# A decode kernel with 80 transfers in place of 88: two head records laid down keys first and loaded together

## The chip, the core and the metric

The kernel runs on one core of one Trainium2 chip. The metric is device time in microseconds (us), the median of the runs. A core has engines that work side by side, each through its own instructions in program order: PE (matrix products), DVE (vector work), ACT (exponentials and copies), POOL, and SP, which here only issues transfers from the chip's memory (HBM) into the core's memory (SBUF). A transfer that SP issues is carried out by 16 DMA engines, each with a part of the 128 partitions, and transfers of one queue are served in the order of their issue. Engines wait for each other, and for transfers, through semaphores; a reader waits for the whole transfer that brings its data.

## The reference, cut to what matters

Two rounds of the same two layers, with the same weights: attention of one new token over the last 1024 positions of a cache with 32 heads, and an MLP with relu. Batch 4, width 640, head size 128, hidden width 1728, all float32.

```python
x = x + _A_ref(_layernorm(x), A_k_cache, A_v_cache, A_wq, A_wo)
x = x + _B_ref(_layernorm(x), B_w1, B_w2)
x = x + _A_ref(_layernorm(x), A_k_cache, A_v_cache, A_wq, A_wo)
x = x + _B_ref(_layernorm(x), B_w1, B_w2)

# _A_ref, W = 1024
q = (x @ wq).reshape(B, Sq, Hq, Dh).transpose(0, 2, 1, 3)
k, v = k_cache[:, :, Sk - W:, :], v_cache[:, :, Sk - W:, :]
p = softmax(einsum("bhqd,bhkd->bhqk", q, k) * Dh ** -0.5)
o = einsum("bhqk,bhkd->bhqd", p, v)
return o.transpose(0, 2, 1, 3).reshape(B, Sq, Hq * Dh) @ wo

# _B_ref
return maximum(x @ w1, 0) @ w2
```

## The kernel before, in words

**Records.** The host lays down all that one head needs as a record of 9472 columns on 128 partitions: its part of `wq` (640 columns, from `WQ`), its keys (4096, from `K` = 640), its values (4096, from `V` = 4736) and its part of `wo` (640, from `WO` = 8832). A record is 4736 KB; "keys of a head" below means columns 0 to `V`, query weights among them, 2368 KB, and "rest" the other half. `wm` holds the MLP's weights in the order of their use.

**Rounds.** The first round (`r` = 0) goes through heads 0 to 31. The last five, 27 to 31, stay in SBUF, and the second round (`r` = 1) begins with them and then takes 0 to 26, so its last three heads are 24, 25 and 26. Five records fit into the tile `store`; a small tile `kept` holds a part of record 26 over the rounds, from column `KEPT` = 6784, and `ring` and a part of record 31's place serve the MLP's weights of the first round.

**Transfers.** A list `items` holds all loads in order, built ahead of the computation (`load`, `run`, `piece`, `group`, `weight`, `ending`). `pump` emits the next loads on SP as soon as the program has released the columns that they overwrite (`done` and `free` release them, at the point of the program where their last reader stands). SP takes them strictly in this order. Most records come five at a time in three transfers (`FIVE`). Towards the end of a round they come in smaller pieces (`ending`), keys ahead of the rest. In the first round's MLP (`MLP_RING`) each load waits for the computation to free its place, and at the start of the second round (`places`) the loads fill the gaps that single released pieces leave. In between, `park` copies four pieces of record 31 into PSUM to make room, and `unpark` copies them back into the freed places of record 27's keys.

**One step of the head loop** (lines 513 to 538). For head `n` PE runs, in this order: the scores of head `n + 1`, the values of head `n`, the query of head `n + 2`, the transposed output of head `n` (`output_T`, into `t_ps`), and head `n`'s projection into `acc` (at once in the second round, except for its last two heads, and held back for the last six of the first). DVE and ACT run the softmax of head `n + 1` beside it. At the last step (`end`) four fills, matrix products whose result nobody reads (`busy`), stand between the values and the last query, and the last head's scores follow that query at once. After the loop come the last two heads' values and projections, layer norm (`center`, `deviation`) and the MLP (`mlp`): the first product over `w1` into `sc_ps`, relu on DVE into `scratch`, the second product over `w2` into `acc`. The final copy and the store end the program.

All operations go through one helper, so the profile puts nearly all of them on its line 102 and tells them apart by their tiles: `misc` is a query, `sc_ps<-store,qT` are scores, `o_ps<-store,scratch` values, `t_ps` the transposed output, `acc<-store,oTs` a projection, `acc<-kept,small` a fill, `acc<-store,scratch` the second product of the second round's MLP.

Of the kernel before, what the change touches and what calls it, by code (L numbers as in the profile page):

```python
# [38 lines left out]
P = 128  # L39
B, D, H, DH, W, FF = 4, 640, 32, 128, 1024, 1728  # L40
# [6 lines left out]
WQ, K, V, WO = 0, D, D + 4 * W, D + 8 * W  # L47
REC = 2 * D + 8 * W
HALF = REC // 2
VH = 2 * W  # L50
# [9 lines left out]
KEPT = WO - 4 * 512  # L60
# [12 lines left out]

IN_RING = [(2176, 4736, "spare", 0), (4736, 6272, "ring", 0), (6272, 8832, "ring", 1536)]

CUTS = [*range(0, K, DH), *range(K, WO, 512), *range(WO, REC + 1, FD)]
W1_SLOT = [[0, 1], [2, 3], [4]]
W2_SLOT = [22, 20, 8, 4]
LATE = 6


FIVE = [REC + 6272, 2 * REC - 3072, 2 * REC - 3200]
LAST_FIVE = [REC + 4736, 2 * REC - 4736, REC, REC]
THREE = [REC + HALF, REC + HALF]
GROUPS = [{h: FIVE for h in range(0, 25, 5)}, {6: THREE, 9: FIVE, 14: FIVE, 19: LAST_FIVE}]


class InOrder:
# [21 lines left out]
def decode_kernel(ctx: ExitStack, tc: tile.TileContext, xf, rec, wm, out):  # L110
# [25 lines left out]
    store = sb.tile([P, FIRST + NS * REC], F32, name="store")  # L136
    kept = sb.tile([P, REC - KEPT], F32, name="kept")
# [39 lines left out]
    LAST = H - NS  # L177


    def home(h, r):  # L180

        if r:
            return FIRST + (h if h >= LAST else h - 6 + LAST) % NS * REC
        return (0 if h < NS else FIRST) + h % NS * REC
# [8 lines left out]
    def load(src, lo, hi, buf, col, parts):  # L193
        items.append((src[:, lo:hi], buf, col, hi - lo, parts))
# [4 lines left out]
    def weight(r, lo, hi, buf, col):  # L199
        buf, col = place(buf, col)  # L200
        load(wm, lo, hi, buf, col, [(("w", r), lo, hi, col)])


    def run(r, lo, hi, buf, col):
        parts = [(("rec", r, h), max(lo - h * REC, 0), min(hi - h * REC, REC), col + max(h * REC - lo, 0))
                 for h in range(lo // REC, (hi - 1) // REC + 1)]
        load(rec, lo, hi, buf, col, parts)

    def piece(r, h, lo, hi, buf="store", col=None):
        run(r, h * REC + lo, h * REC + hi, buf, home(h, r) + lo if col is None else col)  # L210


    def group(r, h, sizes):
        lo = 0
        for size in sizes:
            run(r, h * REC + lo, h * REC + lo + size, "store", home(h, r) + lo)
            lo += size

    def ending(r, hs, late):
        a, b, c = hs[-3:]  # L220
        end = WO if late else REC
        for h, lo, hi in ((a, 0, V), (b, 0, V), (a, V, end), (c, 0, V), (b, V, end), (c, V, WO if late else KEPT)):
            piece(r, h, lo, hi)
        if late:
            for h in hs[-1:] + hs[-LATE:-1]:
                if h == LAST - 1:
                    piece(r, h, WO, REC, "kept", WO - KEPT)
                else:
                    piece(r, h, WO, REC)
# [3 lines left out]
    for h in hs[:-3]:  # L233
        if h in GROUPS[0]:
            group(0, h, GROUPS[0][h])
        if h >= 25:
            piece(0, h, 0, KEPT if h == LAST - 1 else WO if h >= H - LATE else REC)
        if h == LAST - 1:
            piece(0, h, KEPT, WO, "kept", 0)
    ending(0, hs, True)  # L240
    for lo, hi, buf, col in MLP_RING:
        weight(0, lo, hi, buf, col)
# [7 lines left out]
    for lo, hi, buf, col in IN_RING:  # L250
        piece(1, new[0], lo, hi, *place(buf, col))
    places = [("store", old[i] + lo, old[j] + hi) for i, lo, j, hi in (
        (0, 0, 0, K), (0, K + 1024, 0, K + VH), (0, K + VH + 1536, 0, V), (1, 0, 1, K), (1, K, 1, K + VH), (1, K + VH, 1, V),
        (0, V, 0, WO), (2, 0, 2, V), (1, V, 1, REC), (3, 0, 3, V), (2, V, 2, REC), (3, V, 4, FROM))]
    places += [("store", 0, FIRST), ("store", old[4] + FROM, old[4] + REC), ("ring", 0, RING)]
    cuts = [h * REC + x for h in new[1:6] for x in CUTS]
    c, end = new[1] * REC, new[6] * REC
    for buf, lo, hi in places:
        if lo == old[1]:
            piece(1, new[0], WO, REC, buf, lo)  # L260
        elif c < end:
            cut = max(x for x in cuts if x <= min(end, c + hi - lo))
            run(1, c, cut, buf, lo)
            c = cut
    assert c == end
    for h in new[6:-3]:
        if h in GROUPS[1]:
            group(1, h, GROUPS[1][h])
        if not any(g <= h < g + sum(z) // REC for g, z in GROUPS[1].items()):
            piece(1, h, 0, REC)  # L270
    ending(1, hs, False)
    for ks in W1_SLOT:
        weight(1, ks[0] * FF, (ks[-1] + 1) * FF, "store", home(LAST + 1, 0) + ks[0] * FF)
# [54 lines left out]

    def unpark(i):
        b = home(LAST, 0)  # L330
        a = b + (K, K + 512, K + VH, K + VH + 512, K + VH + 1024)[i]
        copy = dve.tensor_copy if i in (0, 2) else act.copy
        copy(store[:, a:a + 512], (sc_ps[1][:, :512], sc_ps[1][:, 512:], o_ps, misc, t_ps)[i])
        live.append(("store", a, a + 512))
        if i == 2:
            dve.memset(o_ps, 0.0)
        if i == 4:
            c = spare
            at["rec", 1, H - 1] = [(0, FROM, "store", c), (FROM, V, "store", a - 512), (V, V + 1024, "store", b + K),
                                   (V + 1024, V + 1536, "store", b + K + VH), (V + 1536, REC, "store", c + V + 1536)]  # L340


    h_ps, warm = sc_ps[0][:, :512], sc_ps[0][:, 512:]
# [55 lines left out]
    def scores(r, h, s, first=False):  # L399
        key = ("rec", r, h)  # L400
        for i in range(2):
            for b in range(B):
                pe.matmul(sc_ps[s][32 * b:32 * b + 32, 512 * i:512 * i + 512], qT[:, b:b + 1].to_broadcast([P, 32]),
                          cols(key, K + 512 * (B * i + b), 512), start=True, stop=True)
            done(key, K + VH * i, K + VH * i + VH)
            if first and i == 0:
                if r:
                    unpark(0)
                deviation(eps_dh, float(DH), True)
                act.activation(unused, eps, AF.Exp)  # L410
                if r:
                    unpark(1)
# [87 lines left out]
    for r in range(2):  # L500
        hs = order[r]
        late = LATE if r == 0 else 2
# [6 lines left out]
        if r:  # L509
            unpark(2)  # L510
            unpark(3)
        weights(0, ((0, 1), (1, 2)))
        for n, h in enumerate(hs[:-2]):
            i = n - (H - late)
# [5 lines left out]
            end = n == H - 3  # L520
# [82 lines left out]
```

## Time and profile before

| | |
|---|---|
| median of 3 runs | 711.71 us (711.58 to 711.9) |
| the profiled execution | 712.25 us |
| its span, first to last instruction | 710.5 us |
| share of the span in which PE, DVE, ACT are busy | 72%, 41%, 14% |
| share of the DMA engines' time that the queue of loads takes | 98.9% |
| read from HBM | 301.34 MB, 424 GB/s over the span |
| mean granted clock of PE | 0.803 of full speed |

The profile is of one execution. Busy shares are means over the whole span and say little where the limit changes from stage to stage: the attention of the first round reaches to about 365 us, its MLP to about 393, the second round's attention to about 693, its MLP to the end. The granted clock is the share of full speed that PE had; here it is 1.00 or 0.50 at any one time. In a timeline row the first number is the start in us from the span's start, the second the length; `x16` joins 16 instructions, and the brackets give the engine's idle time just before and what ended it.

### The profile page before, as it was taken

To read this page: it belongs to the slowest core of one execution; us is meant where nothing else is said; L and a number is where in the kernel's file an instruction comes from. 1 tells how busy PE (TensorE), PEld (TensorE's weight loads), DVE (VectorE), ACT (ScalarE), POOL (GpSimd) and SP (SyncE) were. 2 spreads that over 40 slices of the span, in tenths; PEclk is the share of its full clock that TensorE was granted. 3 is DMA by queue.
4 is the path that set the end of the run, shared out by engine and by line. 5 is a ranking of instruction groups with operands and counts; after the bars stand their busy time and mean duration, and the time that the engine had idled before them with its cause. 6 is when DMAs were issued, how large, how long until landed. Compare 5 with 4: busy or idle time off the path is not lost.

```text
span 710.5 us, 8480 instructions
## 1 busy us (share of the span) xinstructions
PE 513.0 (72%) x3722; PEld 214.0 (30%) x3722; DVE 293.3 (41%) x518; ACT 99.7 (14%) x210; POOL 1.1 (0%) x9
## 2 busy tenths in 40 slices
PE   0777586677584578869888999656584678686986
PEld 0332232232331223333323443222241232332322
DVE  3242353243342343435531775525162243453651
ACT  0110110011010110111120422101010011011110
POOL 0000000000000000000000000000000000000000
PEclk9977787677778776877999999968597677777989
DMA  9999999999999999999999999999999999999996
GB/s 398 439 416 447 425 435 443 414 439 450 418 435 441 424 437 421 423 439 423 430 398 403 412 426 433 445 435 437 431 435 426 438 436 430 432 432 416 433 425 281
DMA packets 12596, 301.96 MB, mean 425 GB/s; under 512 B 1408, under 2 KB 1552, under 8 KB 4624
## 3 DMA queue, kind: packets, MB, share of 16 engines
q1 hardware_dynamic: 12528, 301.42, 98.9%
q8 instruction: 29, 0.48, 0.2%
q14 instruction: 7, 0.06, 0.0%
q10 hardware_dynamic: 32, 0.01, 0.0%
HBM read 301.34 MB, written 0.08 MB: 424 GB/s over the span
## 4 chain that ended last, share of the span: by engine, by line
DMA 72%; PE 23%; DVE 4%; issue 1%; ACT 1%; ACTq 0%; SPq 0%; DVEq 0%
DMA store<-rec 65%; PE sc_ps L102 9%; PE o_ps L102 6%; DMA store<-wm 4%; PE acc L102 3%; PE misc L102 3%; DMA ring<-wm 2%; DVE scratch L102 2%; PE t_ps L102 1%; DVE o_ps L102 1%; ACT oTs L102 1%; DVE small L102 0%; DVE sc_ps L102 0%; ACT sc_ps L102 0%; ACTq L102 0%
## 5 line engine op out<-in xcount | busy, mean ns | idle before, releaser
L102 PE MATMUL sc_ps<-store,qT 128*32 128x512 f32 x1024 | 194.5, 849 | 35.7 <-DMA store<-rec 34.3
L102 PE MATMUL misc<-xT,store 128*128 128x4 f32 x620 | 95.6, 281 | 109.8 <-DMA store<-rec 109.8
L102 DVE TENSOR_REDUCE small<-sc_ps 128x1 f32<-128x1024 f32 x64 | 78.4, 1224 | 181.3 <-PE sc_ps L102 181.2
L102 PE MATMUL o_ps<-store,scratch 128*16 128x512 f32 x960 | 149.5, 701 | 1.7 <-DMA store<-rec 1.4
L102 PEld LDWEIGHTS misc<-xT,store 128*128 128x128 f32 x620 | 90.2, 227 | 166.6 <-DMA store<-rec 119.4
L102 ACT ACTIVATE sc_ps<-sc_ps,small 128x1024 f32<-128x1024 f32 x64 | 69.8, 1091 | 322.6 <-DVE small L102 322.6
L102 DVE STREAM_TRANSPOSE sc_ps<-sc_ps 128x1024 f32<-128x1024 f32 (+1 forms) x70 | 80.8, 1155 | 0.1
L102 PEld LDWEIGHTS sc_ps<-store,qT 128*32 128x32 f32 x1024 | 41.5, 139 | 112.4 <-issue 60.7
L102 PEld LDWEIGHTS o_ps<-store,scratch 128*16 128x16 f32 x960 | 33.8, 117 | 117.4 <-issue 107.8
L102 DVE TENSOR_TENSOR o_ps<-o_ps,of_block 128x512 f32<-128x512 f32 x62 | 43.3, 699 | 50.6 <-PE o_ps L102 50.6
L102 DVE TENSOR_TENSOR qT<-misc,rows 128x4 f32<-128x4 f32 x61 | 9.5, 155 | 112.9 <-PE misc L102 112.9
L102 PE MATMUL acc<-store,oTs 128*4 128x160 f32 x488 | 34.1, 363 | 17.0 <-ACT oTs L102 17.0
L102 DVE TENSOR_REDUCE scratch<-o_ps 128x128 f32<-128x512 f32 x62 | 42.9, 691 | 2.1
L102 ACT COPY oTs<-t_ps 128x4 f32<-128x4 f32 x59 | 9.6, 163 | 207.4 <-PE t_ps L102 207.4
L102 PE MATMUL t_ps<-rows,scratch 128*128 128x4 f32 x118 | 25.8, 289 | 11.3 <-DVE scratch L102 10.3
L102 PEld LDWEIGHTS t_ps<-rows,scratch 128*128 128x128 f32 x118 | 21.9, 231 | 17.4 <-DVE scratch L102 13.1
L102 DVE SCALAR_TENSOR_TENSOR scratch<-sc_ps,small,of_batch 128x128 f32<-128x128 f32 (+1 forms) x70 | 23.7, 339 | 3.5 <-PE o_ps L102 0.9
L102 PE MATMUL acc<-kept,small 128*1 128x328 f32 (+2 forms) x54 | 17.7, 433 | 0.0
L102 PEld LDWEIGHTS acc<-store,oTs 128*4 128x4 f32 x488 | 7.1, 84 | 22.5 <-ACT oTs L102 22.1
L102 ACT ACTIVATION_READ_ACCUMULATOR sc_ps<-sc_ps,small 128x1 f32 x64 | 12.3, 193 | 0.0
L102 DVE RECIPROCAL small<-small 128x1 f32<-128x1 f32 x64 | 9.8, 153 | 2.3 <-ACT sc_ps L102 2.3
L102 PE MATMUL acc<-store,scratch 128*4 128x160 f32 x146 | 6.1, 299 | 3.3 <-DMA store<-wm 3.2
(83 smaller groups left out, 99.8 us busy)
## 6 DMA issues: line engine op xcount, KB each, us to landing
store<-rec SPq DMA_DIRECT2D x14, 7872.0 KB, 27.3
store<-rec SPq DMA_DIRECT2D x7, 7936.0 KB, 29.9
store<-rec SPq DMA_DIRECT2D x4, 7104.0 KB, 30.8
store<-rec SPq DMA_DIRECT2D x11, 2368.0 KB, 36.5
store<-rec SPq DMA_DIRECT2D x3, 4736.0 KB, 25.7
store<-rec SPq DMA_DIRECT2D x2, 4416.0 KB, 29.1
store<-rec SPq DMA_DIRECT2D x3, 2048.0 KB, 40.7
store<-rec SPq DMA_DIRECT2D x1, 4160.0 KB, 21.6
```

The lines of the kernel that those rows point to most:

```text
L102: r = build(*args, **kwargs)
```

## The change

The program's computation is the same; what changes is how the data lies in HBM and in which pieces it is loaded.

- Records 25 and 26 (`PAIR` and `PAIR + 1`) are laid down as one double record: keys of 25, keys of 26, rest of 25, rest of 26. In the first round all of it up to column `KEPT` of record 26 comes in one transfer of 65,024 bytes a partition. In the second round it comes in three: both heads' keys, the rest of 25, and the part of 26's values that `kept` doesn't hold.
- The third last head of a round (29 in the first, 24 in the second) comes in one transfer, up to `WO` in the first round. Before, its keys came first, the next head's keys second and its rest third.
- The last five records that the second round takes in groups (19 to 23) are cut like the others (`FIVE` in place of `LAST_FIVE`): three transfers in place of four.
- In the second round the MLP's `w1` comes in two transfers in place of three.
- At the start of the second round two pairs of places become one place each. `unpark` puts the parked pieces into the first 2560 columns of record 27's keys, behind the query weights, so that the 1536 columns up to `V` are free in one piece; the other pair is record 28's keys.

The longest row of a transfer was 63,488 bytes and is 65,024 bytes; the bytes loaded are the same.

```diff
@@ -73,16 +73,19 @@
 
 IN_RING = [(2176, 4736, "spare", 0), (4736, 6272, "ring", 0), (6272, 8832, "ring", 1536)]
 
+
+PAIR = H - 7
+PAIRED = [(PAIR, 0, V, 0), (PAIR + 1, 0, V, V), (PAIR, V, REC, 2 * V), (PAIR + 1, V, REC, V + REC)]
+
 CUTS = [*range(0, K, DH), *range(K, WO, 512), *range(WO, REC + 1, FD)]
-W1_SLOT = [[0, 1], [2, 3], [4]]
+W1_SLOT = [[0, 1, 2], [3, 4]]
 W2_SLOT = [22, 20, 8, 4]
 LATE = 6
 
 
 FIVE = [REC + 6272, 2 * REC - 3072, 2 * REC - 3200]
-LAST_FIVE = [REC + 4736, 2 * REC - 4736, REC, REC]
 THREE = [REC + HALF, REC + HALF]
-GROUPS = [{h: FIVE for h in range(0, 25, 5)}, {6: THREE, 9: FIVE, 14: FIVE, 19: LAST_FIVE}]
+GROUPS = [{h: FIVE for h in range(0, 25, 5)}, {6: THREE, 9: FIVE, 14: FIVE, 19: FIVE}]
 
 
 class InOrder:
@@ -210,6 +213,11 @@
         run(r, h * REC + lo, h * REC + hi, buf, home(h, r) + lo if col is None else col)
 
 
+    def pair(r, lo, hi):
+        parts = [(("rec", r, h), x + max(lo - a, 0), min(y, x + hi - a), home(PAIR, r) + max(lo, a))
+                 for h, x, y, a in PAIRED if lo < a + y - x and a < hi]
+        load(rec, PAIR * REC + lo, PAIR * REC + hi, "store", home(PAIR, r) + lo, parts)
+
     def group(r, h, sizes):
         lo = 0
         for size in sizes:
@@ -218,10 +226,13 @@
 
     def ending(r, hs, late):
         a, b, c = hs[-3:]
-        end = WO if late else REC
-        for h, lo, hi in ((a, 0, V), (b, 0, V), (a, V, end), (c, 0, V), (b, V, end), (c, V, WO if late else KEPT)):
-            piece(r, h, lo, hi)
-        if late:
+        if not late:
+            piece(r, a, 0, REC)
+            for lo, hi in ((0, 2 * V), (2 * V, V + REC), (V + REC, REC + KEPT)):
+                pair(r, lo, hi)
+        else:
+            for h, lo, hi in ((a, 0, WO), (b, 0, V), (c, 0, V), (b, V, WO), (c, V, WO)):
+                piece(r, h, lo, hi)
             for h in hs[-1:] + hs[-LATE:-1]:
                 if h == LAST - 1:
                     piece(r, h, WO, REC, "kept", WO - KEPT)
@@ -233,10 +244,11 @@
     for h in hs[:-3]:
         if h in GROUPS[0]:
             group(0, h, GROUPS[0][h])
-        if h >= 25:
-            piece(0, h, 0, KEPT if h == LAST - 1 else WO if h >= H - LATE else REC)
-        if h == LAST - 1:
-            piece(0, h, KEPT, WO, "kept", 0)
+        if h == PAIR:
+            pair(0, 0, REC + KEPT)
+            piece(0, h + 1, KEPT, WO, "kept", 0)
+        elif h >= LAST:
+            piece(0, h, 0, WO)
     ending(0, hs, True)
     for lo, hi, buf, col in MLP_RING:
         weight(0, lo, hi, buf, col)
@@ -250,7 +262,7 @@
     for lo, hi, buf, col in IN_RING:
         piece(1, new[0], lo, hi, *place(buf, col))
     places = [("store", old[i] + lo, old[j] + hi) for i, lo, j, hi in (
-        (0, 0, 0, K), (0, K + 1024, 0, K + VH), (0, K + VH + 1536, 0, V), (1, 0, 1, K), (1, K, 1, K + VH), (1, K + VH, 1, V),
+        (0, 0, 0, K), (0, K + VH + 512, 0, V), (1, 0, 1, K), (1, K, 1, V),
         (0, V, 0, WO), (2, 0, 2, V), (1, V, 1, REC), (3, 0, 3, V), (2, V, 2, REC), (3, V, 4, FROM))]
     places += [("store", 0, FIRST), ("store", old[4] + FROM, old[4] + REC), ("ring", 0, RING)]
     cuts = [h * REC + x for h in new[1:6] for x in CUTS]
@@ -328,7 +340,7 @@
 
     def unpark(i):
         b = home(LAST, 0)
-        a = b + (K, K + 512, K + VH, K + VH + 512, K + VH + 1024)[i]
+        a = b + K + 512 * i
         copy = dve.tensor_copy if i in (0, 2) else act.copy
         copy(store[:, a:a + 512], (sc_ps[1][:, :512], sc_ps[1][:, 512:], o_ps, misc, t_ps)[i])
         live.append(("store", a, a + 512))
@@ -337,7 +349,7 @@
         if i == 4:
             c = spare
             at["rec", 1, H - 1] = [(0, FROM, "store", c), (FROM, V, "store", a - 512), (V, V + 1024, "store", b + K),
-                                   (V + 1024, V + 1536, "store", b + K + VH), (V + 1536, REC, "store", c + V + 1536)]
+                                   (V + 1024, V + 1536, "store", b + K + 1024), (V + 1536, REC, "store", c + V + 1536)]
 
 
     h_ps, warm = sc_ps[0][:, :512], sc_ps[0][:, 512:]
@@ -582,6 +594,7 @@
     rec[:, :, K:V] = k.reshape(B, H, 2, W // 2, DH).transpose(1, 4, 2, 0, 3).reshape(H, P, -1)
     rec[:, :, V:WO] = v.reshape(B, H, W // 32, 32, DH).transpose(1, 0, 3, 2, 4).reshape(H, P, -1)
     rec[:, :, WO:] = np.asarray(A_wo).reshape(H, DH, D)
+    rec[PAIR:PAIR + 2] = np.concatenate([rec[h, :, x:y] for h, x, y, _ in PAIRED], 1).reshape(P, 2, REC).swapaxes(0, 1)
     w2 = np.asarray(B_w2)
     blocks = w2.reshape(NB, FQ, D)
     ends = blocks[:, 13 * 32:].reshape(NB, 16, 2, 2 * FD).transpose(0, 2, 1, 3).reshape(P, 2 * FD)
```

## The prediction

> **What bounds the kernel now.** I read the page first, then the windows, then the end of the timeline. On the page: the span, the DMA row of the 40 slices, the queue's share, and the chain by engine.
>
> ```profile
> span 710.5 us, 8480 instructions
> ...
> DMA  9999999999999999999999999999999999999996
> ...
> q1 hardware_dynamic: 12528, 301.42, 98.9%
> ...
> DMA 72%; PE 23%; DVE 4%; issue 1%; ACT 1%; ACTq 0%; SPq 0%; DVEq 0%
> ```
>
> The queue of loads has work in every slice but the last: 98.9% of the span, so all the time in which it carries nothing is 1.1% of 710.5, 7.8 us, most of it the start and the end. Bytes are the bound: 301.42 MB, and the change moves the same bytes. What it can do to the time is three things: fewer packets, a queue that runs dry somewhere, and another end, that is, other work behind the last load that matters. The windows show the rate with long rows and in the stage with the shortest transfers (last column GB/s, before it the DMA share).
>
> ```profile
> 380.00:400.00 20.00, 17.49 (x184) 8.12 (x182) 9.69 (x26) 5.20 (x9) 0.00 (x0) 1.00 0.99 389
> 560.00:600.00 40.00, 29.58 (x193) 13.30 (x197) 14.63 (x25) 4.27 (x10) 0.00 (x0) 0.71 1.01 436
> ```
>
> Then the end, in the timeline of PE, DVE and SP (start, length; in brackets the idle time before it and what ended it).
>
> ```profile
> 663.28 1.28 PE L102 MATMUL misc<-xT,store 128*128 128x4 f32 x10
> ...
> 669.44 1.28 PE L102 MATMUL misc<-xT,store 128*128 128x4 f32 x10
> ...
> 672.05 1.90 PE L102 MATMUL sc_ps<-store,qT 128*32 128x512 f32 x16
> ...
> 675.48 2.37 PE L102 MATMUL acc<-kept,small 128*1 128x328 f32 x8
> ...
> 678.60 1.28 PE L102 MATMUL misc<-xT,store 128*128 128x4 f32 x10 [0.75 <-DMA store<-rec]
> ...
> 680.13 2.50 PE L102 MATMUL sc_ps<-store,qT 128*32 128x512 f32 x16 [0.26 <-DVE qT L102]
> ...
> 700.28 0.19 DVE L102 SCALAR_TENSOR_TENSOR scratch<-scratch,rows 128x32 f32<-128x32 f32 x1
> ...
> 701.22 1.80 PE L102 MATMUL acc<-store,scratch 128*4 128x160 f32 x44 [1.29 <-DMA store<-wm]
> ...
> 704.90 2.79 PE L102 MATMUL acc<-store,scratch 128*4 128x160 f32 x68 [1.88 <-DMA store<-wm]
> ```
>
> Each `misc` row is one head's query. By program order the one at 663.28 is head 24, 669.44 head 25, 678.60 head 26, the last. Head 26 is the first whose query waits for a load (0.75 us), and the four fills ahead of it (675.48) fill a wait. From 678.60 the work is a chain: scores, softmax, values, projections, layer norm, first MLP product, relu, whose last step on DVE ends at 700.47. The second MLP product needs 1.80 + 2.79 = 4.6 us and today waits twice for weights. So **the DMA sets the end by little**: the product ends at 707.69, and relu could end at 707.69 - 4.6 = 703.1 before it counted. The slack of the chain is 2.6 us.
>
> **The change, part by part.**
>
> Packets. Eight transfers fewer are 8 x 144 = 1152 packets of 12528. No row shows a packet's fixed cost alone; the store of the result shows a small transfer by itself, in the DMA view of 708.5 to 709.5.
>
> ```profile
> q1 hardware_dynamic: 144, 0.08, 26.2%
> ```
>
> 144 packets took 0.262 us of each engine. Its 0.082 MB at 436 GB/s are 0.188 us, so 0.074 us are fixed: eight times that is a **gain of 0.6 us**. The bounds are 0 and, from the windows, 20 x (1 - 389/436) = 2.2 us lost among some 14 short transfers, 0.15 each, 1.2 us. It counts only as far as the queue sets the end.
>
> Keys of heads 25 and 26 together, second round. Today the order is keys of 24, keys of 25, rest of 24, keys of 26, rest of 25, half of 26's values; the change makes it all of 24, keys of both, rest of 25, half of 26's values. The bytes up to the end of 26's keys are the same, so the joined keys land when 26's keys land today. But 25's query now waits for that too, two transfers of 2.42 MB at 434 GB/s, 11 us, later. The wait stands at 25's query. Queued behind it on PE are head 23's transposed output and projection, 25's scores, 24's values, the four fills and only then 26's query; on DVE the scaling of 25's query and 24's weights. All of this ran today while the queue brought 26's keys; now it stands **between the landing and the chain**. Its length is query to query. With nothing to wait for and the clock at 1.00 it is 669.44 - 663.28 = 6.2 us. After an idle PE it is longer, as these rows of the same work show, with the granted clock (1.00 or 0.50, the third number from the right) of two stretches.
>
> ```profile
> 580.70 2.30 PE L102 MATMUL misc<-xT,store 128*128 128x4 f32 x10 [4.09 <-DMA store<-rec]
> ...
> 590.23 1.28 PE L102 MATMUL misc<-xT,store 128*128 128x4 f32 x10
> ...
> 616.00 1.88 PE L102 MATMUL misc<-xT,store 128*128 128x4 f32 x10 [4.46 <-DMA store<-rec]
> ...
> 624.74 1.28 PE L102 MATMUL misc<-xT,store 128*128 128x4 f32 x10
> ```
>
> ```profile
> 580.70:587.60 6.90, 6.59 (x36) 3.68 (x40) 1.75 (x4) 0.16 (x1) 0.00 (x0) 0.50 1.01 438
> 681.40:688.10 6.70, 6.27 (x38) 1.48 (x34) 4.08 (x8) 1.37 (x3) 0.00 (x0) 0.50 1.01 431
> ```
>
> After 4.09 us idle the group took 590.23 - 580.70 = 9.5, after 4.46 us 624.74 - 616.00 = 8.7. Here head 24, landed whole some 11 us before the joined keys, is done four or five us before they come, as one warm group is 6.2 us long: I take the mean of the two cold groups, **9.1 us**, bounds 6.2 and 9.5. The fills add 2.3 (row 675.48, less its overlap). In return the chain after 26's query loses its own half-clock stretch: today scores took 2.50 for 1.90, and DVE twice waited for PE, so I take 21.9 - 1.3 = 20.6 us, bounds 20.3 and 21.9. The Trainium skill ("TensorE: Matmul & The Clock Gate", Part 1) says that one busy window of about 3.4 us restores the clock. The trace is slower: 0.50 over 6.9 us above. By the page's window half of 3.4 us would be lost, the group would last about 7.9 us, and the sum would be 1.2 us lower.
>
> The other regrouping (the last five heads of the second round cut like the rest; keys and rest of the third last head whole) moves work before the landing of the joined keys, where PE then waits anyway. If that cover is gone, PE comes late to 25's query but warm, which is the 6.2 end of the bounds.
>
> First round's end. There 25 and 26 come in one transfer (early enough to be worked off), and head 29 comes whole, so its query waits for its values too: 2.10 MB, 4.8 us more than today.
>
> ```profile
> 334.81 1.28 PE L102 MATMUL misc<-xT,store 128*128 128x4 f32 x10
> ...
> 340.38 1.28 PE L102 MATMUL misc<-xT,store 128*128 128x4 f32 x10
> ...
> 346.27 2.37 PE L102 MATMUL acc<-kept,small 128*1 128x328 f32 x8
> 350.06 1.28 PE L102 MATMUL misc<-xT,store 128*128 128x4 f32 x10 [1.43 <-DMA store<-rec]
> ```
>
> The query of 29 (334.81) moves to about 338.5. Warm, two groups of 5.6 us (340.38 - 334.81) and 2.3 of fills bring the last query to 352.0, 2 us late; with one cold group about 4.5 late. The softmax, values and the MLP follow as a chain, and the MLP's weights are loaded into space that this chain frees, so their issues on SP move by the same.
>
> ```profile
> 364.30 0.33 SPq L102 DMA_DIRECT2D store<-wm  x1
> ...
> 368.18 3.13 SPq L102 DMA_DIRECT2D ring<-wm  x3
> ```
>
> ```profile
> store<-wm SPq DMA_DIRECT2D x1, 1080.0 KB, 7.9
> ...
> ring<-wm SPq DMA_DIRECT2D x1, 856.0 KB, 6.6
> ...
> out<-scratch SPq DMA_DIRECT2D x1, 80.0 KB, 1.6
> ```
>
> A transfer on an empty queue lands 1.6 us after its issue, 0.2 of it its bytes. That of 856 KB took 6.6, 2.0 its own bytes, so about 3.2 us of other work stood ahead. A delay of 2 us is hidden by that, one of 4.5 leaves the queue dry for 1.3, and twice in a row at worst 2.8. I take a **loss of 1.0**, bounds 0 and 2.8.
>
> Joined places at the start of the second round. A load waits for the second half of a score pass instead of the first, 0.9 us (half of 1.90), behind as full a queue: nothing; without that cover 0.9 each for two. The joined W1 parts come long before a chain that is now later: nothing.
>
> **The sum**, in the profiled execution's time: 26's keys are worked on from 678.6 today; less seven saved transfers before it (0.5), plus 1.0 of dry queue: 679.1. Plus 9.1 (head 25's group) 688.2, plus 2.3 (fills) 690.5, plus 20.6 (chain to relu) 711.1, plus 4.6 (second product) 715.7, plus what follows it today, 710.5 - 707.7 = 2.8: a span of **718.5**. The profiled execution took 712.25 for a span of 710.5, and the median of the runs is 711.71, 0.54 below it: 718.5 + 1.75 - 0.54 = **719.7 us**, 1.1% slower. With all low ends 678.1 + 6.2 + 2.2 + 20.3 + 4.6 + 2.8 = 714.2, or 715.4; with all high ends 723.4.
>
> **The rivals.**
>
> *The slack takes it* (the other side: not slower). The queue stays the end, and only packets count: 711.71 - 0.6 = 711.1. The point is whether 26's query comes less than about 4 us later (2.6 of slack and 1.3 that the warm chain gives back). For it: the slack exists, and the fills shrink if PE doesn't run them at their length. Against it: even a warm group with its fills is 8.4 us. It needs head 25's keys to be used before 26's, which one transfer with one completion doesn't give. Chance 0.08.
>
> *Joining pays more than packets*: each short transfer costs the queue 0.15 us, and the end stays with the queue: 711.7 - 1.2 = 710.5; if more, it is faster by over 0.2%. The Trainium skill ("DMA: Bandwidth & Descriptors", "Anatomy of one DMA") fits about 2.0 us fixed to a transfer; eight of these would give 695.7. Against it stands the 98.9%: transfers overlap, and 7.8 us are all that is ever idle. Chance 0.04, most of it above 0.2%.
>
> *Only the dry queue*: the second round's end is absorbed, but the MLP stage of the first round loses up to 2.8 us: 711.1 + 2.8 = 713.9. It needs the first rival's condition as well. Chance 0.06.
>
> *The forecast*: 0.82, and its own bounds are the range. The rest, 0.18, is left out of it.
>
> About 0.2% is what a measurement of this kernel can tell from no change: 1.4 us. Faster by more 0.03 (most of the second rival); within it 0.10 (the first, and a little of the second and third); slower 0.87.
>
> **What would show it.** In the changed trace: 25's query waits for `store<-rec` and starts within a microsecond of where 26's starts today; 26's follows 8 to 12 us later without a wait; the second MLP product has no DMA wait ahead of it, and relu ends near 711. The queue's last load lands several us before PE ends. The first round's last query lies 2 to 4.5 us later, and the MLP stage after it shows a lower rate. If 26's query still ends a wait for a load, or the second product still waits for `store<-wm`, the central step is wrong; if the clock is 1.00 through head 25's group, the time is near 716.

## The result: 0.9% slower, and the profile after

| | before | changed |
|---|---|---|
| median of 6 runs | 711.83 us | 718.24 us |
| lowest and highest | 711.58, 712.99 | 717.12, 720.39 |
| profiled execution, its span | 712.25, 710.5 | 719.3, 717.6 |

The ratio is 1.0091, with a 95% interval of 1.008 to 1.0103. The changed kernel also scatters more, by 3.3 us where the kernel before scattered by 1.4 in the same series (in the later ones it spread by 2 to 3, with one run at 717.3).

The page of the changed kernel, span and queue of loads:

```profile
span 717.6 us, 8462 instructions
...
q1 hardware_dynamic: 11376, 301.42, 98.1%
```

1152 packets fewer, the same bytes, and a smaller share of a longer span. The time is not in the packets. Its timeline at the end (PE and DVE; all helper operations stand on line 105 now):

```profile
674.42 1.90 PE L105 MATMUL o_ps<-store,scratch 128*16 128x512 f32 x16
680.60 1.38 PE L105 MATMUL misc<-xT,store 128*128 128x4 f32 x10 [4.27 <-DMA store<-rec]
...
683.20 3.64 PE L105 MATMUL sc_ps<-store,qT 128*32 128x512 f32 x16
686.61 2.82 PE L105 MATMUL o_ps<-store,scratch 128*16 128x512 f32 x16
689.25 2.37 PE L105 MATMUL acc<-kept,small 128*1 128x328 f32 x8
691.55 1.28 PE L105 MATMUL misc<-xT,store 128*128 128x4 f32 x10
...
710.72 4.00 PE L105 MATMUL acc<-store,scratch 128*4 128x160 f32 x112
...
711.26 0.19 DVE L105 SCALAR_TENSOR_TENSOR scratch<-scratch,rows 128x32 f32<-128x32 f32 x1
714.80 0.33 DVE L105 COPY scratch<-acc 128x160 f32<-128x160 f32 x1 [3.35 <-PE acc L105]
```

Read it from the bottom. The second MLP product runs through its 112 steps without a wait for weights; before, it waited for them twice. So the queue no longer sets the end. Going up, nothing waits for a load until the query at 680.60, which is head 25's: PE idled 4.27 us there for the joined keys. Between it and head 26's query (691.55) lie 25's group, 8.65 us, and the fills, 2.30. Before, that query stood at 678.60. The granted clock of the group is the third number from the right in its window:

```profile
680.60:689.20 8.60, 8.29 (x52) 3.34 (x53) 2.97 (x5) 1.20 (x3) 0.00 (x0) 0.60 1.02 433
```

The clock is 1.00 or 0.50, so a mean of 0.60 over 8.6 us is 6.9 us at 0.50.

That leaves the 2 us by which the joined keys came late. In the first round the timeline of PE reads:

```profile
338.49 2.30 PE L105 MATMUL misc<-xT,store 128*128 128x4 f32 x10 [4.87 <-DMA store<-rec]
...
347.66 1.28 PE L105 MATMUL misc<-xT,store 128*128 128x4 f32 x10
...
353.12 2.37 PE L105 MATMUL acc<-kept,small 128*1 128x328 f32 x8
355.42 1.28 PE L105 MATMUL misc<-xT,store 128*128 128x4 f32 x10
```

Head 29's query waits for the whole record, its group runs at half clock (347.66 - 338.49 = 9.2 us where it was 5.6), and the last query is 5.4 us later than before (355.42 against 350.06). The windows after it, of the kernel before and then of the changed one (last column GB/s):

```profile
360.00:370.00 10.00, 9.96 (x97) 3.85 (x91) 2.78 (x9) 3.31 (x6) 0.00 (x0) 0.83 1.01 403
370.00:380.00 10.00, 7.70 (x65) 2.13 (x61) 1.34 (x5) 0.00 (x0) 0.00 (x0) 1.00 1.00 401
380.00:390.00 10.00, 7.98 (x114) 4.28 (x116) 1.29 (x6) 0.00 (x0) 0.00 (x0) 1.00 1.00 396
390.00:400.00 10.00, 9.51 (x74) 3.84 (x66) 8.41 (x20) 5.20 (x9) 0.00 (x0) 1.00 0.98 383
400.00:410.00 10.00, 9.50 (x93) 4.06 (x96) 6.47 (x10) 2.02 (x5) 0.00 (x0) 1.00 1.03 438
```

```profile
360.00:370.00 10.00, 8.58 (x96) 2.93 (x92) 7.00 (x18) 5.42 (x9) 0.00 (x0) 1.00 0.96 380
370.00:380.00 10.00, 7.69 (x65) 2.48 (x65) 1.28 (x5) 0.26 (x1) 0.00 (x0) 1.00 0.94 342
380.00:390.00 10.00, 7.58 (x118) 3.51 (x110) 0.95 (x5) 0.00 (x0) 0.00 (x0) 1.00 0.99 394
390.00:400.00 10.00, 9.50 (x76) 4.00 (x74) 7.16 (x19) 4.00 (x7) 0.00 (x0) 1.00 0.98 375
400.00:410.00 10.00, 9.50 (x88) 4.75 (x88) 7.58 (x14) 3.22 (x7) 0.00 (x0) 1.00 0.99 413
```

From 360 to 380 the rate is 23 + 59 GB/s lower, each for 10 us: 0.82 MB, or 1.9 us at 434 GB/s. From 390 to 410 it is 8 + 25 lower: 0.8 us. The first is the MLP's stage, the second that of the joined places.

### The profile page after: what moved, and what is told of

Read it like the earlier page. It is cut to its first block, busy times and chain, and to the rows that moved or that the text cites. A ratio compares the mean times of both kernels' runs of the same rounds, so it can differ in the third digit from the quotient of the medians.

```text
span 717.6 us, 8462 instructions
## 1 busy us (share of the span) xinstructions
PE 510.2 (71%) x3722; PEld 214.4 (30%) x3722; DVE 293.1 (41%) x518; ACT 99.6 (14%) x210; POOL 1.1 (0%) x9
## 5 line engine op out<-in xcount | busy, mean ns | idle before, releaser
L105 PE MATMUL misc<-xT,store 128*128 128x4 f32 x620 | 97.1, 283 | 116.7 <-DMA store<-rec 116.7
L105 PEld LDWEIGHTS misc<-xT,store 128*128 128x128 f32 x620 | 91.7, 230 | 174.9 <-DMA store<-rec 124.9
```

Source lines behind the costliest of these rows:

```text
L105: r = build(*args, **kwargs)
```

## The experiments

The theory after this: the cost has three parts, the joined keys of 25 and 26 (with 25's group at half clock, and the fills, behind the landing), head 29 whole (the dry queue of the first round's MLP), and perhaps the joined places. The main rival: the other regrouping, larger transfers as such, or a slack that the traces don't show. Each ratio below is to the kernel before on the same chip in the same series; medians of two series differ by some tenths, so times of different series are compared through their ratios. A trace is of one execution: those of e2 and e4 are of the longest of their runs, those of e1, e5 and e9 of the shortest.

| | median us | ratio, 95% interval |
|---|---|---|
| the change | 718.24 | 1.0091, 1.008 to 1.0103 |
| e1 second round's last pieces in the old order | 715.41 | 1.0051, 1.0032 to 1.007 |
| e2 head 29 in two pieces | 716.41 | 1.0064, 1.0043 to 1.0085 |
| e3 both | 713.55 | 1.0017, 1.0006 to 1.0028 |
| e4 before, with head 29 whole | 713.29 | 1.0017, 1.0007 to 1.0027 |
| e5 without the last fills | 715.52 | 1.0054, 1.0037 to 1.007 |
| e6 fills ahead of the landing | 717.56 | 1.0083, 1.0066 to 1.01 |
| e7 last five grouped as before | 718.56 | 1.0097, 1.0082 to 1.0112 |
| e8 29 in two pieces, fills moved | 712.51 | 1.0013, 1.0001 to 1.0026 |
| e9 before, with the joined places | 713.35 | 1.0018, 0.9999 to 1.0037 |
| e10 e3 with the old places | 712.81 | 1.0009, 0.9987 to 1.003 |
| e11 e2 with the old places | 716.87 | 1.0054, 1.0032 to 1.0075 |
| e12 e8 with the old places | 712.47 | 1.0001, 0.9984 to 1.0018 |

**e1: the joined keys undone.**

```diff
-            piece(r, a, 0, REC)
-            for lo, hi in ((0, 2 * V), (2 * V, V + REC), (V + REC, REC + KEPT)):
+            piece(r, a, 0, V)
+            pair(r, 0, V)
+            piece(r, a, V, REC)
+            for lo, hi in ((V, 2 * V), (2 * V, V + REC), (V + REC, REC + KEPT)):
                 pair(r, lo, hi)
```

> The changed kernel, but in the second round the last pieces come in the old order (keys of 24, keys of 25, rest of 24, keys of 26, rest of 25, half of 26's values): 82 transfers. Theory (head 25's group stands between the joined landing and the end, and the queue lost about 2 us net in the first round's MLP besides): the end goes back to the queue, about 2.0 us later than before, 713.8 us, between 712.5 and 714.8; head 25's query comes some 10 us ahead of 26's. Rival (the other regrouping, heads 19 to 23, or larger transfers as such cost the time): stays near 718.

715.41 us: 0.4% less than the change, and 0.6 us over the expected range. Its PE at the end:

```profile
657.28 0.75 PE L105 MATMUL sc_ps<-store,qT 128*32 128x512 f32 x3 [2.75 <-DMA store<-rec]
...
675.62 1.28 PE L105 MATMUL misc<-xT,store 128*128 128x4 f32 x10
...
685.66 1.28 PE L105 MATMUL misc<-xT,store 128*128 128x4 f32 x10
...
707.13 2.75 PE L105 MATMUL acc<-store,scratch 128*4 128x160 f32 x68 [0.48 <-DMA store<-wm]
```

25's query no longer waits for a load, 26's comes 5.9 us sooner than in the change, and the product's second half waits for weights again, for 0.48 us: queue and chain end together. But 25's query stands at 675.62, not at 669.44 as before, and without a wait: PE is late by itself. That is put down to the regrouping of the last five heads, by which head 22's last columns come with head 23: the first row is the end of head 22's scores, which waited for them, and in e4 and e9, which keep the old grouping, 25's query stands at 669.18 and 669.72. Behind the joined keys the delay was covered; here it isn't. No run takes the regrouping alone.

**e2: head 29 in two pieces.**

```diff
-            for h, lo, hi in ((a, 0, WO), (b, 0, V), (c, 0, V), (b, V, WO), (c, V, WO)):
+            for h, lo, hi in ((a, 0, V), (b, 0, V), (a, V, WO), (c, 0, V), (b, V, WO), (c, V, WO)):
                 piece(r, h, lo, hi)
```

> The changed kernel, but in the first round head 29 comes as before, its keys first and its rest after head 30's keys: 81 transfers. Theory (29 whole makes the first round's last query 5 us late, and the MLP's loads run dry for about 2.6 us): the joined keys land about 2.6 us earlier, and the whole is 715.6 us, between 714.6 and 716.6. Rival (the dry stretch is made up later, or comes from the double record in the first round or from the joined places): 718.

716.41 us, as the theory has it (the profiled execution took 718.53, 2.1 us over that median). The windows of its MLP stage and of the places, and head 25's query:

```profile
360.00:370.00 10.00, 9.93 (x99) 3.70 (x92) 2.78 (x9) 2.93 (x6) 0.00 (x0) 0.83 1.02 404
370.00:380.00 10.00, 7.56 (x65) 2.04 (x60) 1.34 (x5) 0.00 (x0) 0.00 (x0) 1.00 0.98 398
...
390.00:400.00 10.00, 9.45 (x72) 4.14 (x68) 8.97 (x20) 5.22 (x10) 0.00 (x0) 1.00 0.95 368
400.00:410.00 10.00, 9.56 (x94) 3.77 (x94) 6.42 (x10) 2.01 (x6) 0.00 (x0) 1.00 1.01 415
```

```profile
679.63 1.28 PE L105 MATMUL misc<-xT,store 128*128 128x4 f32 x10 [4.20 <-DMA store<-rec]
```

The rate of 360 to 380 is back (404 and 398), so head 29 is the cause of the dry stretch. From 390 to 410 it is still 38 GB/s short over 10 us, 0.9 us, and the joined keys come 1.0 us late.

**e3: both undone.** The two diffs above together.

> Both of the two undone, so that only joins stay that delay no query that matters: 83 transfers. Theory: the queue sets the end, with five transfers fewer than before: 711.83 - 0.4 = 711.4 us, between 711.0 and 712.0, and no wait at head 25's query beyond that of before. Rival (joining itself, or the joined places of the second round, costs): 712.5 or more. Rival (joining pays 0.15 us a transfer or more): below 711.1.

713.55 us: the two account for most of the 0.9%, but 0.17% (1.0006 to 1.0028) is left, above the expected range. In its trace the product waits for weights twice, 1.20 and 1.91 us, as in the kernel before, so what is left lies in the queue. The rival in that expectation, that the joined places cost, was taken up in e9 and e10.

**e4: head 29 whole, alone, in the kernel before.**

```diff
-        for h, lo, hi in ((a, 0, V), (b, 0, V), (a, V, end), (c, 0, V), (b, V, end), (c, V, WO if late else KEPT)):
+        heads = [(a, 0, WO)] if late else [(a, 0, V)]
+        heads += [(b, 0, V)] if late else [(b, 0, V), (a, V, end)]
+        for h, lo, hi in heads + [(c, 0, V), (b, V, end), (c, V, WO if late else KEPT)]:
             piece(r, h, lo, hi)
```

> The kernel before with one part of the change alone: head 29 whole in the first round, 87 transfers. Theory: the dry stretch comes from this alone, 2 to 2.6 us, and the queue keeps the end: 714.2 us, between 713.2 and 714.8. Rival (it takes the double record's lateness or the joined places too): 711.8 to 712.5.

713.29 us, 0.17% slower, at the low end. The last query of the first round and the MLP stage:

```profile
353.92 1.28 PE L102 MATMUL misc<-xT,store 128*128 128x4 f32 x10
```

```profile
370.00:380.00 10.00, 7.67 (x64) 2.14 (x63) 1.34 (x5) 0.00 (x0) 0.00 (x0) 1.00 0.94 361
```

A query 3.9 us late costs 40 GB/s over these 10 us, 0.9 us. With the other runs that have 29 whole this gives the size of the cover. The first round's program is the same in the change, e1, e5, e6 and e7, so their lateness differs by the execution alone. The rate is the sum of the windows 360:370 and 370:380, 804 GB/s before, and 787 to 811 in the seven other traces without 29 whole:

| | last query, late by us | GB/s of both windows | lost, us |
|---|---|---|---|
| e5 | 353.31, 3.2 | 400 + 405 | 0 |
| e4 | 353.92, 3.9 | 401 + 361 | 1.0 |
| e7 | 354.73, 4.7 | 393 + 349 | 1.4 |
| e6 | 355.21, 5.2 | 384 + 332 | 2.0 |
| the change | 355.42, 5.4 | 380 + 342 | 1.9 |
| e1 | 355.66, 5.6 | 371 + 339 | 2.2 |

Some 3 us are hidden by the loads that stand ahead in the queue, as the prediction worked out from the landing times; beyond that the queue runs dry.

**e5: without the four fills of the second round.**

```diff
-            if end:
+            if end and not r:
                 for _ in range(4):
                     busy()
```

> The changed kernel without the four fills ahead of the second round's last query. Theory (they stand on the path now): 2.3 us less, 716.0 us, between 715.2 and 716.8. Rival (DVE or the clock holds the last query anyway): 718.

715.52 us: as expected, the fills stand on the path. Its profiled execution is the shortest of its runs (712.65); in it the queue lost nothing in the first round (the table above), and 25's group took 684.67 - 677.58 = 7.1 us for the change's 8.65:

```profile
677.58 1.28 PE L105 MATMUL misc<-xT,store 128*128 128x4 f32 x10 [4.01 <-DMA store<-rec]
...
684.67 1.28 PE L105 MATMUL misc<-xT,store 128*128 128x4 f32 x10
...
704.00 4.00 PE L105 MATMUL acc<-store,scratch 128*4 128x160 f32 x112
```

**e6: seven fills where PE waits for the joined keys.**

```diff
+            if r and n == H - 4:
+                for _ in range(7):
+                    busy()
             query(r, hs[n + 2], n + 2)
```

> The changed kernel with seven more fills in the second round where PE waits for the joined keys (between 23's values and 25's query), about 3.9 us of the 4.3 us that PE idles there. Theory (the idle stretch costs the clock, and head 25's group runs at 0.50): the group shrinks from 8.7 us to about 6.2, the whole to 715.7 us, between 714.8 and 717. Rival (the group is slow for another reason): 718 or a little more.

717.56 us, less than hoped: by its median a miss. The trace tells a part of why (PE; then the issue of the joined keys on SP, and their size and time from issue to landing):

```profile
678.55 4.03 PE L105 MATMUL acc<-kept,small 128*1 128x328 f32 x14
682.50 1.28 PE L105 MATMUL misc<-xT,store 128*128 128x4 f32 x10
...
688.02 2.37 PE L105 MATMUL acc<-kept,small 128*1 128x328 f32 x8
690.32 1.28 PE L105 MATMUL misc<-xT,store 128*128 128x4 f32 x10
```

```profile
652.36 0.33 SPq L105 DMA_DIRECT2D store<-rec  x1
...
store<-rec SPq DMA_DIRECT2D x1, 4736.0 KB, 29.9
```

25's group is 688.02 - 682.50 = 5.5 us now instead of 8.65: the clock was the reason for the long group. But 25's query starts 1.9 us later than in the change, and the fills have little part in that: the joined keys, issued long before the fills, landed at 652.36 + 29.9 = 682.3, 0.2 us before the query; in the change they landed at 651.46 + 29.1 = 680.6. So in this execution the group gave 3.1 us, and a later queue took some 1.7 of them. Whether that holds for the three runs without a trace stays open.

**e7: the last five grouped as before.**

```diff
-GROUPS = [{h: FIVE for h in range(0, 25, 5)}, {6: THREE, 9: FIVE, 14: FIVE, 19: FIVE}]
+GROUPS = [{h: FIVE for h in range(0, 25, 5)}, {6: THREE, 9: FIVE, 14: FIVE, 19: LAST_FIVE}]
```

> The changed kernel with heads 19 to 23 grouped as before (head 22 whole and head 23 whole at the end, 81 transfers). Theory (what it moves lies ahead of the joined keys' landing, where PE waits anyway): no difference, 718.2 us, between 717 and 719.5; PE idles longer ahead of 25's query. Rival (head 22's late columns are the cost): 716 or less.

718.56 us, no difference: with the joined keys in place the regrouping is covered, and 25's query waits for them as it did (680.22). That PE would idle longer ahead of it was not so: it idled 2.41 us there and 1.54 ahead of 24's query (668.99), and 24's group, at a mean clock of 0.61, took 8.8 us.

**e8: the terms together.** The diffs of e2, e5 and e6.

> The changed kernel with its joined keys, but with the three terms taken out: head 29 in two pieces, the four fills moved away from behind the landing, seven fills ahead of it. Theory (the terms add up): 718.2 - 2.6 - 2.3 - 2.5 = 710.8 for the chain, less than the queue's end, so the queue sets it: 711.4 us, between 711.0 and 712.3. Rival (a term is missing, or they overlap): 713 or more.

712.51 us with the keys still joined, 0.2 us over the expected range. The window of 25's group, and the queries of 25 and 26:

```profile
679.20:684.80 5.60, 5.29 (x52) 2.49 (x52) 2.97 (x5) 0.48 (x2) 0.00 (x0) 1.00 0.99 423
```

```profile
679.18 1.28 PE L105 MATMUL misc<-xT,store 128*128 128x4 f32 x10 [0.55 <-DMA store<-rec]
...
684.81 1.28 PE L105 MATMUL misc<-xT,store 128*128 128x4 f32 x10
```

Warm, and with nothing between, 26's query follows 25's by 5.6 us where the change has 10.95.

**e9 to e12: the joined places.** e9 is the kernel before with only the hunks of `places`, `unpark` and its list of pieces; e10, e11 and e12 are e3, e2 and e8 with these hunks undone.

> The kernel before with the joined places at the start of the second round alone (two pairs of transfers joined, and the parked pieces put back to other columns): 86 transfers. Theory, formed after the runs above (the joined loads wait longer for their space than the queue's other work lasts): the queue lies 0.6 to 1.1 us behind from 394 to 406 us on, and the end follows: ratio 1.001 to 1.0015. Rival (the joined places are free, and the rest of the slower time of the kernel with both undone comes from elsewhere): ratio 1.000 or below.

> The changed kernel with all three undone: 29 in two pieces, the second round's last pieces in the old order, the old places: 85 transfers. Theory: the queue sets the end, with three transfers fewer: ratio 0.9995, between 0.9988 and 1.0003. Rival (another part, the double record of the first round, the last five or the joined w1, costs as well): 1.001 or more.

> The changed kernel with 29 in two pieces and the old places, so that of the parts that cost only the joined keys of 25 and 26 stay: 83 transfers. Theory: 25's query waits for the landing at about 678.2 us, 25's group and the fills take about 11, and the whole is some 0.7 us below the kernel with the joined places in it (716.41): 715.7 us, between 714.8 and 716.5. The last load lands several us ahead of the end. Rival (without the queue's losses the slack takes it): below 713.

> As the one before it, with the four fills taken from behind the joined keys' landing and seven put ahead of it: the joined keys stay, PE is warm when they land. Theory: the chain ends ahead of the queue again: ratio 0.9995, between 0.9988 and 1.0006. Rival (head 25's group alone is longer than the slack): 1.002 or more.

e11 shows the joined keys without 29 whole and the joined places: 716.87 us, 1.0054 (1.0032 to 1.0075).

```profile
678.39 2.29 PE L105 MATMUL misc<-xT,store 128*128 128x4 f32 x10 [4.76 <-DMA store<-rec]
...
689.64 1.28 PE L105 MATMUL misc<-xT,store 128*128 128x4 f32 x10
```

Its median is 0.4 us over the expected range, and the rival (the slack takes it) falls: some 0.5% is the price of the joined keys (e10, where they come apart and 24 in pieces, has 1.0009; no run takes 24 whole alone, but in the change PE is not idle ahead of its query, at 670.12). With the fills moved (e12) the ratio is 1.0001 (0.9984 to 1.0018): the same keys, joined, at no cost that can be told.

```profile
679.15 1.28 PE L105 MATMUL misc<-xT,store 128*128 128x4 f32 x10
...
684.78 1.28 PE L105 MATMUL misc<-xT,store 128*128 128x4 f32 x10
```

That is in the expected range, but not quite for the expected reason: the second product runs without a wait for weights, so in this execution the chain set the end, not the queue. And here the fills did run past the landing: the keys were issued at 644.31 and landed 32.5 us later, at 676.8, 2.3 us before the query. Fewer fills were not tried.

The places remain open. Against the two windows of 390 to 410 before (383 + 438 GB/s), the traces of the change, e2, e3, e6, e7 and e8, which join them, are 26 to 42 lower, a loss of 0.6 to 1.0 us; those of e4, e10, e11 and e12, which don't, are 10 to 19 higher. But e1, e5 and e9, which join them too, stand at +7, -14 and +10, e9's times don't tell (1.0018, 0.9999 to 1.0037, over its expected range by its middle), and e3 and e10, or e8 and e12, can't be told apart by their intervals. The four comparisons all point the same way (e9 by 0.18% against before, e2 by 0.10% over e11, e3 by 0.08% over e10, e8 by 0.12% over e12), but none is clear of the noise by itself. If the places cost, it is at most about 1 us, and not in every execution. e10, 1.0009 (0.9987 to 1.003), over its expected range by its middle, doesn't settle either whether another part costs: in its trace 25's query stands at 675.74 without a wait, late as in e1, and the product has no wait for weights. No version tried is faster than the kernel before.

## Why the prediction was right, step by step

The forecast was 719.7 us (715.4 to 723.4), slower. The steps, in the profiled execution:

| step | predicted | measured | from |
|---|---|---|---|
| 25's query, after the landing | 679.1 | 680.6 | its row |
| 25's group | 9.1 | 8.65 | 689.25 - 680.60 |
| the fills | 2.3 | 2.3 | 691.55 - 689.25 |
| 26's query to the end of relu | 20.6 | 19.9 | 711.45 - 691.55 |
| end of relu to the end of the product | 4.6 | 3.3 | 714.72 - 711.45 |
| what follows | 2.8 | 2.9 | 717.6 - 714.72 |
| span | 718.5 | 717.6 | |

- **The wait moved to 25's query and the chain became the end**: right, shown by the traces, by e1 and by e11. The first rival (the slack takes it) asked for a delay below 4 us; 26's query came 13 us later. One sign was missed: 25's query stands 2.0 us behind the place of 26's before, not within a microsecond.
- **Half clock in 25's group**: right, 0.60 over 8.6 us; e6 and e8 keep PE busy ahead of the landing and get 5.5 and 5.6 us. The estimate by the Trainium skill ("TensorE: Matmul & The Clock Gate", Part 1), one busy window of 3.4 us, would have made it 7.9; the trace has 6.9 us at 0.50, twice the window. In e5's trace it was 3.4 us (0.76 over 7.09), one window, and the group took 7.1: both lengths occur.
- **The fills on the path**: right, e5.
- **Dry queue in the first round's MLP**: the mechanism was right (e2, e4), its size 1.9 us for the 1.0 taken, inside the bounds. The lateness was 5.4, over the 4.5 called the cold case, as PE idled 4.87 us ahead of 29's query and the group took 9.2.
- **The joined places at nothing**: doubtful. The profiled execution lost 0.8 us there, about half of the bound that was named (0.9 each for two); whether it is theirs stays open. That bound is not in the range: the high ends of the other terms, added again, give 723.2 already, for the 723.4 that was stated.
- **The last five's regrouping covered**: right as long as the keys are joined (e7); e1 shows what it does without that cover.
- **The second product after relu**: 1.3 us too long. It starts on relu's first part (710.72), before relu ends (711.45); the two durations were added as if it couldn't. With the 0.7 us by which the chain to relu was too long, 26's query had some 6 us of room ahead of the queue's end, not the 4 of the first rival: in e8 and e12 26's query comes 6.2 us later than before (684.81 and 684.78 for 678.60), at 1.0013 and 1.0001. The delay here, 13 us, was far over either.
- **Packets**: 0.6 us of gain, hidden: the queue is not the end any more. No run here measures it. The 2.0 us a transfer that the prediction takes from the Trainium skill ("DMA: Bandwidth & Descriptors", "Anatomy of one DMA") are that section's fit for transfers on the GpSimd path; here SP issues the loads, and no kernel here with fewer transfers is faster than the one before.
- **The joined w1 and the double record of the first round at nothing**: no run takes them alone. e10, which keeps them and the regrouping, has 1.0009 (0.9987 to 1.003).

The late queue (1.5 us more than thought) and the shorter terms at the end (2.4 us less in all) cancelled in part; the span came out 0.9 us shorter than forecast. So the mechanism was right, and that the sum came so near is in part luck.

## What to carry to other kernels

A joined transfer completes as a whole: ask for each part when its first reader wants it, and what that reader's engine has queued behind it, down to the fills. Where a queue of loads sets the time by a small slack, the saving of a transfer is small (0.07 us each by the prediction's estimate; no run here shows it), while a wait moved onto the chain at the end costs what stands behind it beyond that slack: here a group, partly at half clock since PE had idled before it, and the fills, 11 us in all, for a price of some 0.5%. If transfers are to be joined there, work has to be moved with them: fills that kept PE warm in one place belong ahead of the new wait (e12).

## What was not expected of the hardware

The half clock need not begin with the idle stretch, and its length differs. In the changed kernel's trace the clock is 1.00 while PE idles 4.27 us and in the first microsecond of the query; then it is 0.50 through 6.8 us of nearly dense work. In e5's trace the same group has a mean of 0.76 after 4.01 us of idle PE, 3.4 us at 0.50; head 29's group of the changed kernel has 0.53 over 9.11 us, 8.6 at 0.50. The windows of the change, and of e5:

```profile
680.60:681.60 1.00, 1.00 (x9) 1.00 (x10) 0.00 (x0) 0.00 (x0) 0.00 (x0) 1.00 1.01 436
681.60:688.40 6.80, 6.49 (x41) 2.17 (x44) 2.97 (x5) 0.40 (x2) 0.00 (x0) 0.50 1.03 435
```

```profile
677.58:684.67 7.09, 6.78 (x52) 2.72 (x52) 2.97 (x5) 0.47 (x2) 0.00 (x0) 0.76 1.01 426
```

And executions of one program differ in how their half-clock stretches fall: the same first round brought its last query at 353.31 (e5) and at 355.66 (e1), and since the cover ends near 3 us, the queue lost 0 in one and 2.2 us in the other. That the changed kernel's wider scatter comes from this is likely, but only argued.
